# Attention and max-out layer on one core: weights loaded in another order, and the product of w2 and w_out built inside batch 0

## The chip, the cores and the metric

The kernel runs on one core of a Trainium2 chip. The metric is the device time of one execution in microseconds (us), the median of several runs. A core has a matrix engine (PE, with its weight loads PEld shown beside it), a vector engine (DVE), a scalar engine (ACT), a general engine (POOL) and a sync engine (SP) that here only issues transfers. Each engine works through its own list of instructions in order and waits at the head of that list until the data it needs is there. Transfers issued from SP, ACT and POOL are carried by 16 DMA engines.

## The reference

```python
scores = q @ k^T / sqrt(64)                     # batch 8, heads 8, 576 tokens, 64 wide
scores = where(block(i) >= block(j), scores, -1e9)   # blocks of 64 tokens, causal by block
attn   = exp(scores - max) / sum
x      = (attn @ v) with the heads side by side # 4608 tokens x 512
out    = maximum(x @ w1, x @ w2) @ w_out        # w1, w2: 512 x 1024, w_out: 1024 x 512
```

## The kernel before, in words

All products run in bf16 with sums in float32. The max-out layer is rewritten: maximum(x w1, x w2) = x w2 + maximum(x (w1 - w2), 0). The kernel therefore needs d = w1 - w2 (`d_sb`), and M = w2 w_out (`m_sb`), and computes out = x M + maximum(x d, 0) w_out.

The heads are taken as 32 pairs `p`, four pairs per batch; two pairs make a group `g`, whose q and k arrive in one transfer each (`load_qk`, 576 KB). For each group the kernel casts q and k to bf16, transposes them on PE (`transposes`, ps_qT and ps_kT), and copies them out on DVE and ACT. For each pair it then computes scores in pieces (`burst_...` in batch 0, `tile_0`, `tile_1`, `tile_2` later) into two PSUM buffers (`ps_s`), takes exp on ACT (`aT`), zeroes the masked corners with memsets (`mask`, on POOL mostly), multiplies with V (`av`, ps_o; "early" tokens 0 to 255 as `[0, 1]`, "late" ones as `[2, 3, 4]`), and divides by the sums on DVE. `x_out` transposes the result on PE and copies it into `xT`; from batch 1 on a DMA transpose does that instead.

The max-out layer is cut into units that PE works on between the pieces of attention. There are four kinds: `bT_unit` (8 transposes of w2, then one DVE copy into `bT_sb`; four units), `m_unit` (8 matmuls of 256 columns and a DVE copy into `m_sb`; eight units, the first four need the first half of w_out), `h_unit` (4 matmuls and a DVE maximum into `g`), and `y_unit` (12 matmuls into the output). `plan` lists the units in order, each with the tokens it needs. `fill(n)` issues units in that order until a budget of n is spent; a matmul of 512 columns costs 1, one of 256 costs 0.5, a transpose 0.25. `fill_of(g)` sets the budget of a group from the units that are ready. `warm_up(n)` issues n matmuls on zeros, with no result, that only keep PE running.

All other matrix products, transposes and `fill` units take their result from one pool of four PSUM buffers (`ps_m`), handed out in turn: a piece of work may begin only when the one four places before it has been copied out.

The order of everything in batch 0 (groups 0 and 1) and at the start of batch 1 (group 2, pairs 4 and 5) is written out by hand at the end of the program. From group 3 on a loop repeats one pattern: scores of the next pair, a fill, `av` of the pair two before, and so on.

V and the weights are loaded by POOL (`load_v`, `load_w`, `load_wo`), which also converts them to bf16, except w1, that arrives in float32. w2 has no buffer of its own: it lies in a part of `xT` that later batches fill. q and k are loaded by SP; `gated=True` puts a memset on POOL ahead of the transfer, so that it starts only when POOL has come to that point of its list. In the kernel before, POOL loads the first two chunks of V, a quarter of w1, a quarter of w2, the three late chunks of V, then the other quarters in pairs, then w_out, then V of batch 1, then the fourth q and k.

Of the kernel before, what the change touches and what calls it, by code (L numbers as in the profile page):

```python
# [8 lines left out]
FP32 = mybir.dt.float32  # L9
# [5 lines left out]
def kernel(  # L15
# [10 lines left out]
    nc = tc.nc  # L26

    B, H, S, D = q.shape
# [83 lines left out]
    def load_qk(g, queues, gated=False):  # L112
        b, u = divmod(g, GPB)
        for nm, src, queue in (("q", q, queues[0]), ("k", k, queues[1])):
            if queue is None:
                continue
            raws[nm, g] = t = raw.tile([P, 2, RPP * D], FP32, name=f"{nm}raw")
            if gated:
                nc.gpsimd.memset(t[:, 0, :1], 0.0)
            queue.dma_start(  # L120
                out=t[:],
                in_=src[b, 4 * u:4 * u + 4].rearrange(
                    "(s h) (p t) d -> (h p) s (t d)", h=2, t=RPP),
            )

    def cast(nm, g, parts):
        t = raws[nm, g].rearrange("p s (t d) -> p t s d", d=D)
        if (nm, g) not in qk_n:
            qk_n[nm, g] = qkn.tile([P, RPP, 2, D], BF16, name=f"{nm}n")
        n = qk_n[nm, g]  # L130
        for copy, j0, j1 in parts:
            copy(out=n[:, j0:j1], in_=t[:, j0:j1])  # L132

    def load_v(b, c):
        rows = min(P, S - c * P)
        nc.gpsimd.dma_start(  # L136
            out=vv_r[b % NV][P - rows:, c, :, :D],
            in_=v[b, :, c * P:c * P + rows, :].rearrange("h p d -> p h d"),
        )
# [3 lines left out]
    wor = moe_w_out.rearrange("(c p) f -> p c f", p=P)  # L143

    WB = 256
    w1_raw, w2_sb = {}, []
    for j in range(d_ff // WB):
        row, n = (1, j) if j < 3 else (3, 0)
        t0 = 3 * S - 3 * BLK + n * NDM * WB
        w2_sb.append(xT[:, row, t0:t0 + NDM * WB].rearrange("p (c f) -> p c f", c=NDM))  # L150

    def load_w(j, which=(0, 1)):
        fs = slice(j * WB, (j + 1) * WB)
        if 0 in which:
            w1_raw[j] = wraw.tile([P, NDM, WB], FP32, name="w1raw")
            nc.gpsimd.dma_start(out=w1_raw[j][:], in_=w1r[:, :, fs])
        if 1 in which:
            nc.gpsimd.dma_start(out=w2_sb[j], in_=w2r[:, :, fs])

    def diff_w(j):  # L160
        fs = slice(j * WB, (j + 1) * WB)
        nc.vector.tensor_sub(d_sb[:, :, fs], w1_raw[j][:], w2_sb[j])  # L162

    WH = d_model // 2

    def load_wo(i):
        ds = slice(i * WH, (i + 1) * WH)
        nc.gpsimd.dma_start(out=wo_sb[:, :, ds], in_=wor[:, :, ds])  # L168
# [8 lines left out]
    nc.vector.memset(zeros[:], 0.0)  # L177
    nc.scalar.activation(out=warm[:], in_=warm[:], func=AF.Exp)
    load_qk(1, (SP, SP))
    load_qk(2, (SP, None))  # L180
    make_identity(nc, ident)
    for r in range(NV):
        nc.vector.memset(vv_r[r][:, :, :, D:D + 1], 1.0)
# [6 lines left out]
    cast("k", 0, ((act, 0, 5), (dve, 5, RPP)))  # L190
    for c in range(2):
        load_v(0, c)
    load_w(0, (0,))
    cast("q", 1, ((pool, 7, RPP),))
    cast("k", 1, ((pool, 0, 7),))
    load_w(0, (1,))


    done_tokens = [0]
# [23 lines left out]
    def bT_unit(j):  # L223
        pt = ps_m.tile([P, 2, NDM, P], BF16, name="ps_bT", tag="m")
        for i in range(2):
            for c in range(NDM):
                nc.tensor.transpose(pt[:, i, c, :], w2_sb[j][:, c, i * P:(i + 1) * P], ident[:])
                if i == 1 and c == NDM - 1:
                    nc.vector.tensor_copy(
                        out=bT_sb[:, 2 * j:2 * j + 2, :],  # L230
                        in_=pt.rearrange("p i c d -> p i (c d)"))
                yield

    def m_unit(i, c):
        ds = slice(i * WH, (i + 1) * WH)
        pt = ps_m.tile([P, WH], FP32, name="ps_M", tag="m")
        for f in range(NFF):
            nc.tensor.matmul(  # L238
                pt[:], bT_sb[:, f, c * P:(c + 1) * P], wo_sb[:, f, ds],
                start=(f == 0), stop=(f == NFF - 1),  # L240
            )
            if f == NFF - 1:
                nc.vector.tensor_copy(out=m_sb[:, c, ds], in_=pt[:])
            yield
# [40 lines left out]
    def plan():  # L285
        def h(i, f):
            t0, w = spans[i]
            units.append((h_unit(i, f), t0 + w, w / SPAN, NDM))

        def y(i, s, last=False):  # L290
            t0, w = spans[i]
            if last:
                units.append((y_last(i, s), t0 + w, 0.333, 3 * NY))
            else:
                units.append((y_unit(i, s), t0 + w, 1.0, NY))

        for i in range(NSPAN):
            for f in range(NFF):
                h(i, f)
                if i == 0 and f % 2:  # L300
                    units.append((bT_unit(f // 2), 0, 0.25, 2 * NDM))
                if i > 2 and f % 2 == 0 and f // 2 < tiles[i - 1]:
                    y(i - 1, f // 2)
            if i == 1:
                for n in range(2 * NDM):
                    units.append((m_unit(n // NDM, n % NDM), 0, 0.5, NFF))
                for j in range(2):
                    for s in range(tiles[j]):
                        y(j, s)
        n = tiles[-1]  # L310
        for s in range(n):
            y(NSPAN - 1, s, s == n - 1)
# [25 lines left out]
    def warm_up(n):  # L338
        pw = ps_m.tile([P, SPAN], FP32, name="ps_w", tag="m")
        for _ in range(n):  # L340
            nc.tensor.matmul(pw[:], zeros[:, :P], zeros[:], start=True, stop=True)  # L341
# [4 lines left out]
    def transposes(nm, g, copies):  # L346
        n = qk_n.pop((nm, g))
        pts = [ps_m.tile([P, RPP, NP], BF16, name=f"ps_{nm}T", tag="m") for _ in range(2)]
        for j in range(RPP):
            for i in range(2):  # L350
                r = slice(i * NP, (i + 1) * NP)
                nc.tensor.transpose(  # L352
                    pts[i][:, j, :], n[r, j].rearrange("p s d -> p (s d)"), ident[r, r],
                )

        def copy_out(which=(0, 1), part=(0, NP), copy=None):
            p0, p1 = part
            for i in which:
                t = (qT_r if nm == "q" else kT_r)[(2 * g + i) % NT]
                (copy or copies[i])(  # L360
                    out=t[:, p0 * RPP:p1 * RPP].rearrange("q (p j) -> q p j", j=RPP),
                    in_=pts[i][:, :, p0:p1].rearrange("q j p -> q p j"),
                )
        return copy_out
# [12 lines left out]
    def pad_keys(p):  # L377
        nc.gpsimd.tensor_copy(
            out=kz_r[p % NT].rearrange("p (a c) -> p a c", c=BLK)[:, 0:3:2],
            in_=kT_r[p % NT][:, S - 3 * BLK:].rearrange("p (a c) -> p a c", c=BLK)[:, 0:3:2],  # L380
        )
# [31 lines left out]
    def burst_q1(p):  # L413
        burst(p, ((0, QCUT, 320), (1, QCUT, 192)), 384)

    def burst_q2(p):
        burst(p, ((1, 448, P), (2, QCUT, 320), (4, 512, BLK)), 896)

    def burst_q3(p):
        burst(p, ((3, 384, 192),), 1408)  # L420

    def masks_p(p, eng=None):
        for a in (0, 256):
            mask(p, a, eng)

    def masks_q(p, eng=None):
        for a in (1024, 1408):
            mask(p, a, eng)
# [160 lines left out]
    burst_p(1)  # L589
    warm_up(2)  # L590
    masks_p(1)
    for c in range(2, NCH):
        load_v(0, c)
    load_qk(2, (None, SP), gated=True)
    load_w(1)
    cq = transposes("q", 1, (dve, dve))
    burst_q1(0)
    ck = transposes("k", 1, (dve, dve))
# [15 lines left out]
    masks_p(3, nc.vector)  # L614
    burst_q2(0)
    av(2, [0, 1])
    warm_up(2)
    x_out(0, 0, 2, (act, act))
    av(3, [0, 1])
    diff_w(0)  # L620
    burst_q1(1)
    warm_up(2)
    cast("q", 2, ((pool, 0, RPP),))
    masks_q(0)
    load_w(2)
    burst_q2(1)
    x_out(1, 0, 2)
    warm_up(2)
    burst_q3(1)
    masks_q(1)  # L630
    load_w(3)
    fill(4)
    burst_q1(2)
    transposes("q", 2, (dve, act))()
    burst_q2(2)
    av(0, [2, 3, 4])
    burst_q3(2)
    masks_q(2)
    cast("k", 2, ((pool, 0, RPP),))
    load_wo(0)  # L640
    load_wo(1)
    av(1, [2, 3, 4])
    burst_q1(3)
    burst_q2(3)
    av(2, [2, 3, 4])
    transposes("k", 2, (dve, act))()
    burst_q3(3)
    masks_q(3)
    pad_keys(4)
    pad_keys(5)  # L650
    for c in range(NCH):
        load_v(1, c)
    load_qk(3, (SP, SP), gated=True)
    x_out(0, 2, NCH)
    fill(2)
    diff_w(1)
    outs = tile_0(4), tile_1(4)
    av(3, [2, 3, 4])
    region(*outs)
    x_out(1, 2, NCH)  # L660
    fill(4)
    diff_w(2)
    fill(2)
    region(tile_2(4), tile_0(5))
    fill(4)
    diff_w(3)
    fill(2)
    region(tile_1(5), tile_2(5))
    fill(4)
    fill(2)  # L670
    cast("q", 3, ((pool, 0, RPP),))
    cast("k", 3, ((pool, 0, RPP),))
    n = fill_of(GPB)
# [86 lines left out]
```

The softmax here doesn't subtract the row's maximum and nothing guards it: scores larger than these inputs give would overflow.

## Time and profile before

| what | value |
|---|---|
| time, median of 3 runs | 260.99 us (260.82 to 261.92) |
| span of the profiled execution | 259.2 us |
| PE busy | 244.8 us (94%) |
| DVE, ACT, POOL busy | 137.6, 141.3, 109.8 us |
| TensorE clock granted | 1.0 of full speed throughout |
| read from HBM, written to it | 34.60 MB, 9.44 MB |

Busy time is the time in which an engine had an instruction at work. PE is the busiest by far, so the places where PE is not busy, or is busy with matmuls on zeros, are where time can be found. The matmuls overlap in the pipeline, so that the mean length of one in the table of groups (0.2 to 0.4 us) is longer than the step from one to the next.

### The profile page before, as it was taken

What the parts mean: (1) busy time and instruction counts of PE and PEld (TensorE: products, weight loads), DVE (VectorE), ACT (ScalarE), POOL (GpSimd) and SP (SyncE); (2) the same over time, 40 slices, a digit from 0 to 9 for tenths busy, and PEclk for the clock granted to TensorE, in tenths of its full rate; (3) what the DMA queues carried; (4) which work ended last, traced back from release to release, by engine and by line L of the source; (5) the groups of instructions that cost most, each with busy time, mean ns of one, the idle gap of its engine ahead of it and who ended that gap; (6) DMA issues with size and microseconds to landing.
All of it is one profiled execution on the core that took longest, in us unless ns stands there. A gap on an engine that the chain in (4) does not pass through costs nothing.

```text
span 259.2 us, 7161 instructions
## 1 busy us (share of the span) xinstructions
PE 244.8 (94%) x2949; PEld 139.4 (54%) x2983; DVE 137.6 (53%) x301; ACT 141.3 (55%) x198; POOL 109.8 (42%) x274
## 2 busy tenths in 40 slices
PE   8688799999999999999999999999999999999995
PEld 3346566856555545454646464646464655444444
DVE  4967996646584518451855185518550853453200
ACT  2798552766665766576657665776577431100111
POOL 2987914475638163816381638263823010000000
DMA  7999998789579995998599949984986122202122
GB/s 245 317 204 310 194 241 146 280 73 275 111 184 250 135 195 136 238 149 215 129 236 139 179 163 239 141 208 139 90 106 116 44 51 83 83 0 81 43 104 99
DMA packets 71265, 41.30 MB, mean 159 GB/s; under 512 B 53568, under 2 KB 58048, under 8 KB 71232
## 3 DMA queue, kind: packets, MB, share of 16 engines
q1 hardware_dynamic: 28544, 31.27, 41.4%
q0 software_dynamic: 42272, 8.92, 38.2%
q10 hardware_dynamic: 416, 0.66, 0.7%
q8 instruction: 23, 0.38, 0.6%
q14 instruction: 10, 0.08, 0.1%
HBM read 34.60 MB, written 9.44 MB: 170 GB/s over the span
## 4 chain that ended last, share of the span: by engine, by line
PE 85%; DMA 5%; POOL 3%; issue 2%; ACT 2%; DVE 1%; POOLq 0%; ACTq 0%
PE ps_y L257 35%; PE ps_h L215 22%; PE ps_o L479 10%; PE ps_s L371 8%; DMA qraw<-in_q_dram 5%; PE ps_M L238 3%; PE ps_qT L352 2%; PE ps_kT L352 2%; POOL vv L136 1%; ACT aT L395 1%; PE ps_y L272 1%; DVE qn L132 1%; PE ps_w L341 1%; PE ps_s L389 1%; POOL wo_sb L168 1%
## 5 line engine op out<-in xcount | busy, mean ns | idle before, releaser
L395 ACT ACTIVATE aT<-ps_s 128x1024 bf16<-128x1024 f32 (+2 forms) x100 | 95.9, 996 | 28.6 <-PE ps_s L371 26.6
L215 PE MATMUL ps_h<-xT,d_sb 128*128 128x512 bf16 (+3 forms) x306 | 67.4, 357 | 2.7 <-DVE d_sb L162 1.2
L257 PE MATMUL ps_y<-wo_sb,g 128*128 128x512 bf16 x275 | 69.1, 379 | 0.4 <-issue 0.3
L220 DVE TENSOR_SCALAR g<-ps_h 128x512 bf16<-128x512 f32 (+3 forms) x80 | 50.8, 636 | 30.2 <-PE ps_h L215 28.4
L400 POOL MEMSET aT<- 64x128 bf16 x124 | 22.4, 199 | 85.1 <-ACT aT L395 84.4
L485 DVE RECIPROCAL rec<-ps_o 128x4 f32<-128x4 f32 (+1 forms) x64 | 12.0, 188 | 62.7 <-PE ps_o L479 61.9
L215 PEld LDWEIGHTS <-d_sb 128*128 128x128 bf16 x320 | 29.1, 98 | 30.1 <-issue 2.7
L479 PEld LDWEIGHTS <-aT 128*128 128x128 bf16 x960 | 37.2, 98 | 13.5 <-issue 0.8
L262 ACT COPY y<-ps_y 128x512 f32<-128x512 f32 x31 | 18.2, 587 | 44.8 <-PE ps_y L257 32.6
L257 PEld LDWEIGHTS <-g 128*128 128x128 bf16 x280 | 25.9, 98 | 29.7 <-issue 1.9
L479 PE MATMUL ps_o<-vv,aT 128*128 128x65 bf16 x960 | 39.8, 194 | 0.0
L257 PE MATMUL ps_y<-m_sb,xT 128*128 128x512 bf16 x128 | 36.5, 380 | 1.2 <-issue 0.8
L136 POOL DMA_DIRECT2D vv<-in_v_dram x40 | 33.6, 847 | 1.6 <-issue 1.2
L371 PE MATMUL ps_s<-qT,kT 64*128 64x64 bf16 (+6 forms) x344 | 31.0, 280 | 1.9 <-ACT kT L360 0.7
L486 DVE TENSOR_TENSOR xp<-ps_o,rec 128x256 bf16<-128x256 f32 (+1 forms) x64 | 31.4, 491 | 2.2
L360 ACT COPY qT<-ps_qT 128x576 bf16<-128x576 bf16 (+1 forms) x17 | 10.3, 614 | 20.0 <-PE ps_qT L352 20.0
L132 POOL CAST qn<-qraw 128x1152 bf16<-128x1152 f32 (+1 forms) x16 | 17.0, 1061 | 8.7 <-DMA qraw<-in_q_dram 8.7
L257 PEld LDWEIGHTS <-xT 128*128 128x128 bf16 x140 | 12.2, 98 | 15.1 <-issue 3.5
L371 PEld LDWEIGHTS <-kT 64*128 64x128 bf16 x344 | 12.2, 94 | 11.0 <-issue 6.2
L132 POOL CAST kn<-kraw 128x1152 bf16<-128x1152 f32 (+1 forms) x15 | 17.1, 1141 | 1.4 <-DMA kraw<-in_k_dram 1.3
L360 ACT COPY kT<-ps_kT 128x576 bf16<-128x576 bf16 x15 | 9.6, 639 | 14.6 <-PE ps_kT L352 14.6
L207 POOL COPY g<-g 128x512 bf16<-128x512 bf16 x8 | 4.9, 613 | 20.7 <-DVE g L220 20.3
(57 smaller groups left out, 160.8 us busy)
## 6 DMA issues: line engine op xcount, KB each, us to landing
qraw<-in_q_dram SPq DMA_DIRECT2D x16, 576.0 KB, 4.1
out_dram<-y SPq DMA_DIRECT2D x35, 256.0 KB, 3.2
kraw<-in_k_dram SPq DMA_DIRECT2D x15, 576.0 KB, 5.4
vv<-in_v_dram POOLq DMA_DIRECT2D x32, 128.0 KB, 5.2
w1raw<-in_moe_w_dram POOLq DMA_DIRECT2D x4, 512.0 KB, 8.7
xT<-in_moe_w_dram POOLq DMA_DIRECT2D x4, 256.0 KB, 9.1
wo_sb<-in_moe_w_out_dram POOLq DMA_DIRECT2D x2, 512.0 KB, 9.0
kraw<-in_k_dram ACTq DMA_DIRECT2D x1, 576.0 KB, 5.5
```

Of the source, the lines that this page charges most:

```text
L132: copy(out=n[:, j0:j1], in_=t[:, j0:j1])
L136: nc.gpsimd.dma_start(out=vv_r[b % NV][P - rows:, c, :, :D], in_=v[b, :, c * P:c * P + rows, :].rearrange("h p d -> p h d"),)
L215: nc.tensor.matmul(pt[:, :w], d_sb[:, c, f * P:(f + 1) * P], xT[:, c, t0:t0 + w], start=(c == 0), stop=(c == NDM - 1),)
L220: nc.vector.tensor_scalar_max(g[:, f, m:m + w], pt[:, :w], 0.0)
L257: nc.tensor.matmul(py[:], lhs, rhs, start=(n == 0), stop=(n == len(terms) - 1),)
L262: (dve if i < 2 else act)(out=y[:], in_=py[:])
L360: (copy or copies[i])(out=t[:, p0 * RPP:p1 * RPP].rearrange("q (p j) -> q p j", j=RPP), in_=pts[i][:, :, p0:p1].rearrange("q j p -> q p j"),)
L371: nc.tensor.matmul(ps[:, hh, col:col + w], kT[r, k0:k0 + P], qT[r, q0:q0 + w], start=True, stop=True,)
L395: nc.scalar.activation(out=aT_r[p % NA][:, :, a0:a0 + w], in_=ps[:, :, :w], func=AF.Exp, scale=scale,)
L400: (eng or nc.gpsimd).memset(aT_r[p % NA][BLK:, :, a0:a0 + BLK], 0.0)
L479: nc.tensor.matmul(po[:, gi, hh, :], a[:, hh, a0:a0 + P], vv[:, c, h0 + 2 * hh, :], start=(mm == 0), stop=(mm == n_mm - 1),)
L486: nc.vector.tensor_mul(xp[:, :, ts[0]:ts[0] + n, p % 2].rearrange("q s t d -> q t s d"), po[:, :, :, :D], rec[:, :n].to_broadcast([P, n, 2 ...
```

## The change

The change reorders the loads and the work of batch 0. POOL now loads, after the first two chunks of V, the whole of w2 in two halves of 1 MB read each, half of w_out, the late chunks of V, the other half of w_out, and two quarters of w1; then come the third q and k (both gated behind the masks of pair 1), the last two quarters of w1, three chunks of V of batch 1, the fourth q and k, and the last two chunks of V. The units of w2's transposes and of M move to the head of the plan, in front of all others. They take the place of three pairs of matmuls on zeros, and stand between the scores and the late values of batch 0. The subtractions d = w1 - w2 and the first h units move behind M.

```diff
+    WC = d_ff // 2
+    w2_sb = [xT[:, row, 3 * S - 3 * BLK:3 * S - 3 * BLK + NDM * WC].rearrange(...) for row in (1, 3)]
+    def load_w2(i):
+        nc.gpsimd.dma_start(out=w2_sb[i], in_=w2r[:, :, i * WC:(i + 1) * WC])
...
-    load_qk(2, (SP, None))
...
-    load_w(0, (0,))
+    load_w2(0)
     cast("q", 1, ((pool, 7, RPP),))
     cast("k", 1, ((pool, 0, 7),))
-    load_w(0, (1,))
+    load_w2(1)
...
+        for n in range(NFF // 2):
+            units.append((bT_unit(n), 0, 0.25, 2 * NDM))
+        for n in range(2 * NDM):
+            units.append((m_unit(n // NDM, n % NDM), 0, 0.5, NFF))
...
     masks_p(1)
+    load_wo(0)
     for c in range(2, NCH):
         load_v(0, c)
-    load_qk(2, (None, SP), gated=True)
-    load_w(1)
+    load_wo(1)
+    load_w1(0)
+    load_w1(1)
...
     av(2, [0, 1])
-    warm_up(2)
+    fill(2)
     x_out(0, 0, 2, (act, act))
     av(3, [0, 1])
-    diff_w(0)
     burst_q1(1)
-    warm_up(2)
-    cast("q", 2, ((pool, 0, RPP),))
+    fill(2)
     masks_q(0)
-    load_w(2)
     burst_q2(1)
     x_out(1, 0, 2)
-    warm_up(2)
+    fill(2)
     burst_q3(1)
     masks_q(1)
-    load_w(3)
-    fill(4)
+    load_qk(2, (SP, SP), gated=True)
+    fill(2)
     burst_q1(2)
-    transposes("q", 2, (dve, act))()
     burst_q2(2)
+    fill(4)
+    fill(4)
+    burst_q3(2)
+    load_w1(2)
+    masks_q(2)
+    burst_q1(3)
+    load_w1(3)
+    fill(4)
+    fill(4)
+    burst_q2(3)
     av(0, [2, 3, 4])
...
     burst_q3(3)
     masks_q(3)
+    cast("q", 2, ((pool, 0, RPP),))
+    cast("k", 2, ((pool, 0, RPP),))
+    for c in range(3):
+        load_v(1, c)
+    load_qk(3, (SP, SP), gated=True)
+    for c in range(3, NCH):
+        load_v(1, c)
+    av(1, [2, 3, 4])
+    av(2, [2, 3, 4])
+    x_out(0, 2, NCH)
+    diff_w(0)
+    fill(4)
+    fill(4)
+    transposes("q", 2, (dve, act))()
+    av(3, [2, 3, 4])
+    fill(4)
+    transposes("k", 2, (dve, act))()
     pad_keys(4)
     pad_keys(5)
...
     diff_w(1)
...
     x_out(1, 2, NCH)
     fill(4)
+    region(tile_0(4), tile_1(4))
+    fill(4)
     diff_w(2)
-    fill(2)
     region(tile_2(4), tile_0(5))
     fill(4)
     diff_w(3)
-    fill(2)
+    fill(4)
     region(tile_1(5), tile_2(5))
     fill(4)
```

More of the change, by code (lines that the diff above doesn't have):

```diff
@@ L145, with load_w1 @@
     WB = 256
[L146 to L158, printed above, removed]
+    w1_raw = {}
+    WC = d_ff // 2
+    w2_sb = [
+        xT[:, row, 3 * S - 3 * BLK:3 * S - 3 * BLK + NDM * WC].rearrange("p (c f) -> p c f", c=NDM)
+        for row in (1, 3)]
+    def load_w1(j):
+        w1_raw[j] = wraw.tile([P, NDM, WB], FP32, name="w1raw")
+        nc.gpsimd.dma_start(out=w1_raw[j][:], in_=w1r[:, :, j * WB:(j + 1) * WB])
+    def load_w2(i):
+        nc.gpsimd.dma_start(out=w2_sb[i], in_=w2r[:, :, i * WC:(i + 1) * WC])
     def diff_w(j):
-        fs = slice(j * WB, (j + 1) * WB)
-        nc.vector.tensor_sub(d_sb[:, :, fs], w1_raw[j][:], w2_sb[j])
+        n = j * WB % WC
+        nc.vector.tensor_sub(
+            d_sb[:, :, j * WB:(j + 1) * WB], w1_raw[j][:], w2_sb[j * WB // WC][:, :, n:n + WB])
     WH = d_model // 2
@@ L225, in bT_unit @@
         for i in range(2):
+            f = 2 * j + i
             for c in range(NDM):
-                nc.tensor.transpose(pt[:, i, c, :], w2_sb[j][:, c, i * P:(i + 1) * P], ident[:])
+                nc.tensor.transpose(pt[:, i, c, :], w2_sb[f // (NFF // 2)][:, c, f % (NFF // 2) * P:(f % (NFF // 2) + 1) * P], ident[:])
                 if i == 1 and c == NDM - 1:
@@ L299, in plan @@
                 h(i, f)
-                if i == 0 and f % 2:
-                    units.append((bT_unit(f // 2), 0, 0.25, 2 * NDM))
                 if i > 2 and f % 2 == 0 and f // 2 < tiles[i - 1]:
@@ L304, in plan @@
             if i == 1:
-                for n in range(2 * NDM):
-                    units.append((m_unit(n // NDM, n % NDM), 0, 0.5, NFF))
                 for j in range(2):
@@ L616 @@
     av(2, [0, 1])
-    warm_up(2)
+    fill(2)
     x_out(0, 0, 2, (act, act))
     av(3, [0, 1])
-    diff_w(0)
     burst_q1(1)
-    warm_up(2)
-    cast("q", 2, ((pool, 0, RPP),))
+    fill(2)
     masks_q(0)
-    load_w(2)
     burst_q2(1)
     x_out(1, 0, 2)
-    warm_up(2)
+    fill(2)
     burst_q3(1)
     masks_q(1)
-    load_w(3)
+    load_qk(2, (SP, SP), gated=True)
+    fill(2)
+    burst_q1(2)
+    burst_q2(2)
     fill(4)
-    burst_q1(2)
-    transposes("q", 2, (dve, act))()
-    burst_q2(2)
-    av(0, [2, 3, 4])
[L637 to L646, printed above, removed]
+    fill(4)
[7 more added lines that the diff above has]
+    burst_q2(3)
+    av(0, [2, 3, 4])
     burst_q3(3)
     masks_q(3)
+    cast("q", 2, ((pool, 0, RPP),))
[15 more added lines that the diff above has]
+    transposes("k", 2, (dve, act))()
     pad_keys(4)
     pad_keys(5)
[L651 to L654, printed above, removed]
-    fill(2)
     diff_w(1)
-    outs = tile_0(4), tile_1(4)
-    av(3, [2, 3, 4])
-    region(*outs)
     x_out(1, 2, NCH)
     fill(4)
+    region(tile_0(4), tile_1(4))
+    fill(4)
     diff_w(2)
-    fill(2)
     region(tile_2(4), tile_0(5))
@@ L666 @@
     diff_w(3)
-    fill(2)
+    fill(4)
     region(tile_1(5), tile_2(5))
     fill(4)
-    fill(2)
     cast("q", 3, ((pool, 0, RPP),))
```

## The prediction

> **What bounds the kernel now.** I read the page's head first, then stretches of the span, then the order of PE and the waits of the stretches where PE is not full. The page:
>
> ```profile
> span 259.2 us, 7161 instructions
> PE 244.8 (94%) x2949; PEld 139.4 (54%) x2983; DVE 137.6 (53%) x301; ACT 141.3 (55%) x198; POOL 109.8 (42%) x274
> ...
> PE   8688799999999999999999999999999999999995
> ```
>
> PE is the bound, and its gaps lie in the first six or seven slices, some 40 us. The busy time by stretch (time; then busy us of PE, PEld, DVE, ACT, POOL; clock; share and GB/s of the DMA engines):
>
> ```profile
> 15.50:26.00 10.50, 9.54 (x202) 6.53 (x201) 7.56 (x19) 9.65 (x14) 8.05 (x15) 1.00 1.35 272
> 26.00:34.50 8.50, 6.10 (x99) 4.37 (x96) 7.76 (x15) 4.96 (x7) 6.12 (x17) 1.00 1.56 188
> 34.50:44.00 9.50, 8.80 (x104) 6.73 (x105) 7.59 (x16) 2.71 (x5) 2.92 (x7) 1.00 1.15 173
> 44.72:56.28 11.56, 11.51 (x191) 8.38 (x193) 6.44 (x17) 7.55 (x10) 6.29 (x20) 1.00 0.80 202
> 56.28:67.41 11.13, 10.81 (x184) 6.44 (x180) 6.71 (x15) 7.55 (x10) 6.17 (x15) 1.00 0.99 186
> ```
>
> PE idles 0.96, 2.40 and 0.70 us in the first three rows: 4.06 us between 15.5 us and 44.72, where group 3 begins. Before 15.5 PE's list is the same in both kernels. From group 3 on PE idles about 2%, nearly all of it "issue". PE's own waits between 26 and 41 us:
>
> ```profile
> PE ps_xe L517 <- DVE xp L486: 1.2, 1, 1.2
> PE ps_h L215 <- DVE d_sb L162: 1.2, 2, 0.6
> ...
> PE ps_qT L352 <- POOL qn L132: 0.6, 1, 0.6
> ```
>
> PE waits for attention's division (late values follow each other with nothing between), for d (w1 comes last), and for the fourth q. M comes only after that, when PE is already full:
>
> ```profile
> 15.53 0.59 PE L341 MATMUL ps_w<-zeros 128*128 128x512 bf16 x2
> ...
> 16.89 0.60 PE L341 MATMUL ps_w<-zeros 128*128 128x512 bf16 x2
> ...
> 41.42 1.58 PE L238 MATMUL ps_M<-wo_sb,bT_sb 128*128 128x256 bf16 x13
> ```
>
> The third zero pair runs at 17.87. All real work is the same in both kernels, so the gain can only be zero work removed and idle time filled.
>
> [...] the third k, issued at 14.15 behind POOL's loads, took 8.0 us to land; a q of the same 576 KB issued at 42.30, when little else ran, took 3.7. [...] w2's transposes replace the zero matmuls; but the trace has them at 219 ns each, eight in 0.54 us to the next start, with the clock at 1.00, so I charge nothing. [...] I count steps from start to start and not lengths.
>
> **The ceiling.** Steps from the order of PE before: 8 transposes of w2 0.54 us; an M matmul 0.123 (12 in 1.48); a zero matmul 0.216; a y matmul 0.215 (6 in 1.30).
> At the start of group 3 the old kernel has done 25 of 64 M matmuls; the new order has done all 64 and 2 y matmuls. That lead is 39 x 0.123 + 2 x 0.215 = 5.23 us. The old PE was busy 25.16 of the 29.22 us to 44.72. The new work is 25.16 - 6 x 0.216 + 5.23 = 29.09 us. With no idle time group 3 would start at 44.6 with 5.23 us less to do: a ceiling of 1.30 + 4.06 = 5.36 us. From pair 10 on, the two orders hold the same fills per piece, so what is won by then stays won.
>
> **w2 and w_out early.** In the old trace the second V chunk landed at 12.7 us, with the third q (landed 10.9) beside it. Without that q I put it at 11.7. For 1 MB read of weights the queue took 1.7 us (second w_out half, 32.5 to 34.2), 2.6 (first) or 2.7 (last quarters of w1 and w2, 27.2 to 29.9). At 2.4 each, w2 lands at 14.1 and 16.5, the first w_out half at 18.9; at 12.7 and 2.7 each it is 20.8. PE wants the halves of w2 at 15.5 and 17.9, and w_out at 19.75. So I take no wait; the upper end is 1.0 us. The late V follows (0.9 us a chunk, 18.3 to 20.0 before): about 21.6, wanted at 24.4. The second w_out half at about 24 to 25.5, wanted at 27.5. None waits.
>
> **bT and M between the scores.** DVE copies of bT (0.69 each) come between divisions; the last is done near 20.0, and M reaches those columns at 20.5. ACT is the busy engine here (9.65 of 10.5), and now gets scores a little later: exp for pair 3 ends near 25.9, as before (26.0). That costs PE nothing, since it has M to do. Small waits for a division and for PSUM: 0.2 us.
>
> **From 27 to 40 us.** Here I laid PE's new list and DVE's beside each other with the old steps: on DVE a division (reciprocal and product) 0.76 us, x copies 0.6, each of four subtractions 1.22, an M copy 0.42, a q or k copy 0.75, a maximum 0.43; on PE late values 0.84, an M unit 0.98, an h pair 0.9. What PE then waits for:
> Late values of pair 3: their PSUM is that of M's fifth unit, which DVE copies only after the first subtraction (28.5 to 29.7): ready at 30.1, wanted at 29.75, 0.4.
> Transposes of x for group 1: those values divided, and M's seventh unit copied: 0.15.
> M's last unit: its buffer is the third k's, copied at 33.1, wanted at 32.7: 0.45.
> First h units: x copies stand behind the second subtraction on DVE, done 34.9: 0.1.
> Scores of pair 5: two score buffers, an exp of 0.97 us each, so PE waits for ACT: 0.6.
> Last quarter's h units: fourth subtraction done at 39.4, wanted at 39.2: 0.2.
> The sum is 1.9, with the 0.2 above 2.1 us, against 4.06 in the old kernel.
>
> **Third and fourth q, k and V.** POOL reaches the gate of the third q and k after pair 1's exp, at 19.8. With 8 us to land as in the old case, q is there at 27.8 and k at about 29; casts (1.15 each) end at 29.0 and 30.4; PE wants them at 29.5 and 32. The wait is nothing, up to 1.75 us if they queue behind all the weights. Behind the casts on POOL stand V of batch 1 (0.84 us an issue) and the fourth q, k: issued at 33 in place of 31.34. Its landing was 7.6 and 9.1 us later; at 40.6 and 42.1, cast by 43.3, against PE's wish at 43 and 45. V was there at 43.6, and is wanted at about 47. No wait in the forecast.
>
> **Group 3 and 4, given back.** The lead makes `fill_of` smaller: the fills there were 39 M and 12 y matmuls (7.38 us) and 30 y (6.45), and are 20 y in each (4.30). Of the old 11.56 and 11.13 us PE keeps 8.5 and 9.0, and ACT still has 7.55. At the end of a group ACT has a copy 0.64, two exps 0.97 and a corner 0.27 = 2.85 us in line, PE only 0.55 of scores and 6 fills of 0.215, then a first score piece of 0.25: 2.1. So a wait of about 0.75 at group 5; at group 4 the x transposes (0.5) cover most. I take 0.8 in all; the bounds are 0 and 1.6.
>
> **Sum.** 5.36 - 2.1 - 0.8 = 2.46 us; 260.99 - 2.46 = 258.5.
>
> **Rivals.**
> First, everything is hidden: DVE keeps up and groups 3 and 4 do not wait. Idle of 0.9 us stays, 5.36 - 0.9 = 4.5, so 256.5. For it: POOL's cast of the third q leaves a contested time, and PE waits in groups 3 and 4 have so far been nil. Against: DVE is 7.76 of 8.5 us busy already in that stretch.
> Second, late loads: w_out at 20.8 costs 1.0 us, and the fourth q and k 1.1 more, so 260.6, no change that counts. For it: the DMA engines are loaded throughout, 11 MB in 32 us. Against: the bytes ahead of w_out are fewer than what preceded it.
> Third, slower: POOL's list stalls at the third q's cast. If q lands at 30, its cast ends at 31.2 (1.75 us of PE), and V of batch 1 is issued until 36.6; with its old 13 us to land, it comes at 49.6, 1.6 us after it is wanted. With w_out's 1.0: 258.5 + 4.35 = 262.9. For it: POOL works in order, and everything behind that cast waits. Against: the 13 us held weights ahead in the queue that are now gone.
>
> **How the numbers follow.** Forecast 0.58, everything hidden 0.12, late loads 0.19, stall 0.11. The first two are faster by over 0.5% (under 259.7): 0.70. Late loads are within: 0.19. Stall is slower (over 262.3): 0.11. The range reaches from the first rival to a little beyond the late loads, 256.4 to 260.9, and leaves out the stall.
>
> **What would show it.** Right: the zero pairs gone; ps_M between 19.7 and 34 us; group 3's first scores at 46 to 47; PE idle near 2 us between 15.5 and there, released by DVE and ACT; a short wait of ps_s on ACT at the start of group 5; the loop's steady part unchanged. Wrong: PE waiting for a DMA, first ps_M on w_out, or ps_qT on POOL's cast; ps_o waiting for V of batch 1; or PE waits in groups 3 and 4 well above 1 us.

## The result, and the profile after

| | before | after |
|---|---|---|
| time, median | 260.9 us (4 runs, 260.73 to 261.92) | 263.6 us (4 runs, 263.17 to 264.53) |
| ratio | | 1.010 (95% interval 1.0062 to 1.0138) |
| span of the profiled execution | 259.2 us | 262.8 us |

The forecast was 258.5 us and faster; the kernel became 2.7 us slower, outside the range of 256.4 to 260.9. The page after, by its head, the row of PE in 40 slices, and a row that the page of the kernel before did not have, the granted clock:

```profile
span 262.8 us, 7139 instructions
...
PE 245.1 (93%) x2943; PEld 138.8 (53%) x2977; DVE 137.5 (52%) x301; ACT 141.8 (54%) x198; POOL 108.4 (41%) x273
...
PE   7578769998999999999999999999999999999995
...
PEclk9999998999999999999999999999999999999999
```

Six matmuls on zeros are gone, and PE is busy for 0.3 us more. Slices of low PE busy time reach to about 40 us as before, and in the seventh (39.4 to 46.0 us) the clock was below full. Busy time by stretch (time; PE, PEld, DVE, ACT, POOL; clock; DMA share and GB/s):

```profile
15.50:26.00 10.50, 8.74 (x124) 6.43 (x122) 5.56 (x14) 7.30 (x10) 4.61 (x13) 1.00 1.62 218
26.00:33.60 7.60, 6.25 (x149) 5.30 (x147) 5.43 (x13) 2.15 (x3) 1.54 (x3) 1.00 0.97 337
33.60:38.66 5.06, 2.60 (x50) 1.95 (x46) 3.06 (x6) 0.64 (x1) 3.36 (x4) 1.00 0.16 23
38.66:42.28 3.62, 3.62 (x25) 1.72 (x25) 2.15 (x7) 2.00 (x3) 2.88 (x9) 0.54 1.68 133
42.28:51.80 9.52, 9.25 (x107) 6.21 (x107) 9.09 (x18) 5.75 (x8) 3.52 (x11) 1.00 0.79 165
51.80:60.72 8.92, 8.60 (x159) 5.36 (x162) 4.86 (x12) 6.72 (x9) 5.62 (x14) 1.00 0.76 267
60.72:70.34 9.62, 8.94 (x173) 5.42 (x169) 6.18 (x14) 7.56 (x11) 6.59 (x17) 1.00 1.37 224
```

PE's idle time to the start of group 3 (51.80) is 1.76 + 1.35 + 2.46 + 0.27 = 5.84 us, where the old kernel had 4.06 and the forecast 2.1. On top, in the fourth row PE is "busy" throughout at 0.54 of its clock, which is 3.62 x 0.46 = 1.67 us lost. The waits of PE between 12 and 75 us:

```profile
PE ps_kT L352 <- POOL kn L132: 1.9, 1, 1.9
PE ps_o L479 <- DVE m_sb L243: 1.2, 1, 1.2
...
PE ps_M L238 <- DMA wo_sb<-in_moe_w_out_dram: 0.9, 1, 0.9
PE ps_s L371 <- ACT aT L451: 0.9, 2, 0.5
PE ps_bT L227 <- DMA xT<-in_moe_w_dram: 0.7, 1, 0.7
PE ps_M L238 <- ACT kT L360: 0.6, 1, 0.6
```

The largest in this trace is the third k. POOL, which casts it, stood still for it 4.4 us, and V of batch 1 and the fourth q and k stood behind it (POOL's timeline):

```profile
29.77 1.14 POOL L132 CAST qn<-qraw 128x1152 bf16<-128x1152 f32 x1 [1.67 <-DMA qraw<-in_q_dram]
35.30 1.15 POOL L132 CAST kn<-kraw 128x1152 bf16<-128x1152 f32 x1 [4.38 <-DMA kraw<-in_k_dram]
36.39 1.77 POOL L136 DMA_DIRECT2D vv<-in_v_dram  x2
```

That k was issued at 21.12 and took 14.0 us. In the old kernel the third k, issued at 14.15, took 8.0. The lower clock shows in PE's timeline: the same six score matmuls take 1.04 us at 38.66 (clock 0.50) and 0.61 at 51.80 (1.00).

```profile
38.66 1.04 PE L371 MATMUL ps_s<-qT,kT 64*128 64x512 bf16 x6
...
51.80 0.61 PE L371 MATMUL ps_s<-qT,kT 64*128 64x512 bf16 x6
```

The sum of the profiled run: ceiling 5.36, less idle 5.84, less clock 1.67, less 1.55 given back from group 3 to the start of group 5 (below), is -3.7 us; the two spans differ by 3.6. The median of the four runs is 0.9 us better than this profiled run (264.53): the other three had a mean clock of 1.00 and took 263.17 to 263.80. So the clock adds to the profiled run, but it is not what makes the median slow.

### The profile page after: what moved, and what is told of

Its sections match the earlier page's. It is cut to its first block, busy times and chain, and to the rows that moved or that the text cites. A ratio compares the mean times of both kernels' runs of the same rounds, so it can differ in the third digit from the quotient of the medians.

```text
span 262.8 us, 7139 instructions
## 1 busy us (share of the span) xinstructions
PE 245.1 (93%) x2943; PEld 138.8 (53%) x2977; DVE 137.5 (52%) x301; ACT 141.8 (54%) x198; POOL 108.4 (41%) x273
## 4 chain that ended last, share of the span: by engine, by line
PE 81%; DMA 10%; ACT 4%; issue 2%; POOL 1%; SPq 0%; ACTq 0%; POOLq 0%
PE ps_y L257 34%; PE ps_h L214 24%; PE ps_o L479 10%; PE ps_s L371 7%; DMA kraw<-in_k_dram 5%; DMA xT<-in_moe_w_dram 3%; ACT aT L395 3%; PE ps_kT L352 2%; DMA qraw<-in_q_dram 2%; PE ps_qT L352 2%; PE ps_y L272 1%; PE ps_s L389 1%; ACT kT L360 1%; POOL vv L136 1%; POOL kn L132 0%
## 5 line engine op out<-in xcount | busy, mean ns | idle before, releaser
L214 PE MATMUL ps_h<-xT,d_sb 128*128 128x512 bf16 (+3 forms) x307 | 68.1, 361 | 1.4 <-issue 1.0
L479 PE MATMUL ps_o<-vv,aT 128*128 128x65 bf16 x960 | 39.6, 194 | 1.2 <-DVE m_sb L243 1.2
L371 PE MATMUL ps_s<-qT,kT 64*128 64x64 bf16 (+6 forms) x344 | 31.8, 285 | 2.6 <-ACT aT L451 0.9
L360 DVE COPY kT<-ps_kT 128x576 bf16<-128x576 bf16 (+2 forms) x19 | 12.9, 685 | 1.9 <-PE ps_kT L352 1.9
```

Of the source, the lines that this page charges most:

```text
L214: nc.tensor.matmul(pt[:, :w], d_sb[:, c, f * P:(f + 1) * P], xT[:, c, t0:t0 + w], start=(c == 0), stop=(c == NDM - 1),)
L360: (copy or copies[i])(out=t[:, p0 * RPP:p1 * RPP].rearrange("q (p j) -> q p j", j=RPP), in_=pts[i][:, :, p0:p1].rearrange("q j p -> q p j"),)
L371: nc.tensor.matmul(ps[:, hh, col:col + w], kT[r, k0:k0 + P], qT[r, q0:q0 + w], start=True, stop=True,)
L479: nc.tensor.matmul(po[:, gi, hh, :], a[:, hh, a0:a0 + P], vv[:, c, h0 + 2 * hh, :], start=(mm == 0), stop=(mm == n_mm - 1),)
```

## The experiments

All stand beside runs of the kernel before on the same chip (medians 260.9 to 261.0). The edits of e1 to e4, e7 and e8 are made in the changed kernel; e5 builds on e1.

**e1, the third q at the start again.**

```diff
     load_qk(1, (SP, SP))
+    load_qk(2, (SP, None))
...
-    load_qk(2, (SP, SP), gated=True)
+    load_qk(2, (None, SP), gated=True)
```

> One part undone: the third q is loaded at the very start again, ungated, as in the kernel before; the third k stays behind the masks of pair 1. Theory A (the DMA engines ran below their rate from 9 to 12 us once the third q was taken out of the opening, and the third k then lands at 35.1 us because it queues with everything that was pushed back): 590 KB leave the crowded stretch, about 1.5 us at the 390 KB/us read there, so the third k lands near 33.5, w2's first half still near 16.5 to 17.5, and the time falls by 1 to 2.5 us against the changed kernel (263.6), to about 261 to 262.5. Theory B (the third k is late because its gate opens only at 20.6 us, whatever else is in the queue): the third k still lands after 34.5 and the time stays within 0.7 us of 263.6.

Measured: 260.83 us, ratio to before 0.9992 (0.9975 to 1.0009). The third k was issued at 20.84 and landed at 31.0, not 35.1. The waits of PE from 12 to 75 us:

```profile
PE ps_M L239 <- DMA wo_sb<-in_moe_w_out_dram: 1.3, 1, 1.3
...
PE ps_s L372 <- ACT aT L452: 0.9, 2, 0.5
...
PE ps_o L480 <- DMA vv<-in_v_dram: 0.7, 1, 0.7
PE ps_M L239 <- ACT kT L361: 0.3, 1, 0.3
```

PE no longer waits for the third k, and the whole 2.7 us is back, though PE now waits longer for w_out and also for V. The 1.2 us wait for a copy of M is gone as well: w1's first quarter, for which the first subtraction waits, lands at 29.8 in place of 31.2. Where one transfer stands in the queue is worth the result of the whole change. The gain is above Theory A's 1 to 2.5; that the freed 1.5 us of transfer moved the landing by 4.2 us was not expected.

**e2, the gate of the third q and k earlier.**

```diff
     load_wo(1)
+    load_qk(2, (SP, SP), gated=True)
     load_w1(0)
...
     masks_q(1)
-    load_qk(2, (SP, SP), gated=True)
```

> One part moved: the gate of the third q and k stands right after the issue of w_out's second half, ahead of w1, in place of behind the masks of pair 1 (issue near 16 us, not 20.7). Theory A (the third k's landing sets the stretch from 33 to 42 us, and its gate and the four quarters of w1 decide it): the third k lands between 24 and 28 us, PE no longer waits for it (1.9 us) or for its copy (0.6), the clock stays at 1.00, and the time falls by 2.5 to 4.5 us from 263.6, to 259 to 261; the price is w_out's first half up to 1 us later. Theory B (the waits for w2, w_out and d set the time, and the third k only comes on top of them by chance): PE's wait moves to w_out and d, and the time falls by under 1 us.

Measured: 262.97 us, ratio 1.006 (1.0037 to 1.0082). In the profile, a run of 261.28 us, the third q landed at 23.5, k at 26.3, and PE did not wait for them; it waited 0.8 us for w_out and 0.7 for late V. But of 20 runs only 6 had a mean clock of 1.00 (median 261.2); 11 had 0.993 or 0.994 (median 263.2), and three had 0.987 (264.9 to 266.5) and are not in the ratio. Theory A is right on the landing, near on the time in the runs at full clock (259 to 261 expected), and wrong that the clock stays. The profile is of a run at full clock, so where the clock falls in this version was not seen.

**e3, zero matmuls while PE waits.**

```diff
     fill(4)
+    warm_up(9)
     transposes("k", 2, (dve, act))()
```

> Nine matmuls on zeros (about 1.9 us at the 0.216 us step) are added in the changed kernel ahead of the third k's transposes, where PE idles 1.9 us for that k. Theory A (the granted clock falls to half for 3.6 us because PE idled just before, worth 1.7 us in a run where it happens): the clock is 1.00 in every run, first scores of group 3 come 1 to 1.7 us earlier than the 51.8 of the profiled run, and the median falls by 0.3 to 1.5 us, since only one of four runs of the changed kernel shows a mean clock below 1.00. Theory B (the clock is not a matter of the idle time there): the mean clock still falls in some runs and the median stays within 0.3 us, or rises by the zeros that are not hidden.

Measured: 264.20 us, ratio 1.0117 (1.0084 to 1.0151): no gain. In its profile PE idled 1.74 of the 4.00 us from 29 to 33, and the clock was at half before PE came to the zeros:

```profile
29.00:33.00 4.00, 2.26 (x49) 1.89 (x47) 2.45 (x4) 0.64 (x1) 1.14 (x1) 0.94 0.94 325
33.00:36.00 3.00, 3.00 (x18) 1.83 (x16) 1.29 (x4) 0.00 (x0) 1.75 (x2) 0.50 0.10 29
```

So the zeros, which start at 34.9, came too late: the clock fell behind a wait of 1.3 us for a copy of M, before PE reached them. The other three runs had mean clocks of 0.998 to 1.00 and took 263.3 to 265.2, no less than the changed kernel. That fits Theory B. This run does not say what keeping PE busy would have been worth, only that this place did not do it.

**e4, the first subtraction later.**

```diff
-    diff_w(0)
     fill(4)
     fill(4)
     transposes("q", 2, (dve, act))()
+    diff_w(0)
```

> The first subtraction stands behind two M units and the third q's transposes in place of ahead of them, so that the copies of M no longer wait on the vector engine for w1. Theory A (the third k's landing at 35.1 us ends this stretch, and the wait ahead of it, 1.2 us of the late values of pair 3 for a copy of M, is swallowed by it): the wait at 31.7 goes, the wait for the third k grows by as much, and the time stays within 0.7 us of 263.6. Theory B (each wait adds to the time by itself): the time falls by about 1.2 us, to 262.4.

Measured: 263.16 us, ratio 1.0088 (1.0053 to 1.0122), 0.4 us below the changed kernel. The 1.2 us wait is gone in the profile, a wait of 1.4 us for the third k remains. The time stays within 0.7 us, as Theory A has it, but its reason is not shown: the wait for the k became shorter and not longer, since the gate opened 0.6 us earlier in that run and the k landed at 33.1. And all four runs had a mean clock of 0.993, where three of the changed kernel's four had 1.00. In the two traces, each with one fall of the clock, group 3 starts at 50.07 here and at 51.80 there. So this run does not decide between the theories.

**e7, w1 behind the third k.** The last two quarters of w1 are issued behind the casts. The question is whether transfers issued at about the same time as the k, or after it, hold it up.

```diff
     burst_q3(2)
-    load_w1(2)
...
     burst_q1(3)
-    load_w1(3)
...
     cast("k", 2, ((pool, 0, RPP),))
+    load_w1(2)
+    load_w1(3)
```

> In the changed kernel the last two quarters of w1 are issued behind the casts of the third q and k, so that these two transfers no longer share the DMA engines with them. Theory A (the third k takes 14 us [...]): the third k lands 2 to 3 us sooner, near 32.5, PE's wait for it falls below 0.7 us, and the time falls by 1 to 2.5 us from 263.6. Theory B (the third k waits only for what was issued ahead of it: V, w_out, the first half of w1 and the third q): it still lands near 35, and the time does not fall.

Measured: 262.80 us, ratio 1.0068 (1.0051 to 1.0085). The third k was issued at 20.32 and landed at 31.9, 3.2 us before the changed kernel's. Of that, 0.8 us is the earlier issue; the k took 11.6 us in place of 14.0. In e3, e4 and e8, which leave these loads as they are, it took 12.6 to 13.8, so 1.0 to 2.4 us are this edit's. The two transfers that were moved had been issued at 20.82 and 24.72 on POOL's queue, one 0.3 us ahead of the k (21.12, on SP's) and one 3.6 us after it; which of the two held it up was not tried apart. Theory A is right on the landing, wrong on the time: PE's wait for the k is gone, yet the time fell by only 0.8. A wait that had not existed took its place:

```profile
PE ps_s L389 <- POOL kz L378: 1.8, 1, 1.8
```

POOL now issues two quarters of w1 (1.5 us), besides V of batch 1 and the gate of the fourth q and k, ahead of the padded keys that the first corner scores need.

**e8 and e5, what groups 3 and 4 give back.** The middle fills of these two groups are halved, so that more is left for the end; e8 is the changed kernel, e5 is e1.

```diff
-        lo, hi = max(3, n // 18), n * 2 // 9
+        lo, hi = max(3, n // 18), n // 9 if g < 5 else n * 2 // 9
```

In the changed kernel, PE's timeline at the start of groups 4 and 5 showed these two lines (the scores' last part, with the wait ahead of it in brackets):

```profile
61.62 0.40 PE L371 MATMUL ps_s<-qT,kT 64*128 64x64 bf16 x4 [0.47 <-ACT aT L451]
...
71.24 0.40 PE L371 MATMUL ps_s<-qT,kT 64*128 64x64 bf16 x4 [0.47 <-ACT aT L451]
```

> The fills of groups 3 and 4 are moved as in e5, in the changed kernel itself. Theory A (what groups 3 and 4 give back stands apart from the late loads): the time falls by the same 0.5 to 1.3 us as e5 against e1, to 262.3 to 263.1. Theory B (it is part of one chain with the late loads): no fall, or a different one.

> The third q early as in e1, and in groups 3 and 4 the two fills in the middle are halved, so that the fill at the end of the group is larger (10 y matmuls' worth in place of 6). Theory A (groups 3 and 4 give back about 1.5 us, because the scores at the start of groups 4 and 5 wait 0.5 us each for exps still in line on the scalar engine, with too little fill at the end of the group): the waits of 0.47 us at the start of groups 4 and 5 go, and the time falls by 0.5 to 1.3 us from e1's 260.8, to 259.5 to 260.3. Theory B (the scalar engine's work per group, 7.55 us of 9, sets the pace wherever the fill stands): the wait moves to the middle of the group and the time stays within 0.4 us of e1.

Measured: e8 262.43 us, ratio 1.0057 (1.0038 to 1.0075), 1.2 below the changed kernel; e5 260.06 us, ratio 0.9961 (0.9947 to 0.9975), 0.8 below e1. Both 0.47 us waits are gone in both, and the times are as Theory A has them. But the traces do not show that the whole gain comes from there. A new wait stands in group 3, for POOL's cast of the fifth q, where the middle fill was made smaller (e8, then e5):

```profile
53.35 0.44 PE L352 MATMUL ps_qT<-ident,qn 64*128 64x64 bf16 x18 [0.94 <-POOL qn L132]
50.52 0.44 PE L353 MATMUL ps_qT<-ident,qn 64*128 64x64 bf16 x18 [0.62 <-POOL qn L132]
```

From the first scores of group 3 to those of the second pair of group 5, the changed kernel takes 23.68 us and e8 23.60; e1 takes 23.67 and e5 23.27. In e8 nearly all the difference between the two traces lies before group 3, where nothing was edited: group 3 starts at 49.71, with no fall of the clock and 4.69 us of idle PE in place of 5.84. In that trace PE does not wait for the third k (landed at 33.6), but 2.0 us for w_out and 1.4 for a copy of M. So which of the late loads holds PE differs from run to run of the same code, and why e8's median is 1.2 lower stays open in part.

**e6, the third q behind the first V.** As e1, but q is gated behind the two V chunks.

```diff
         load_v(0, c)
+    load_qk(2, (SP, None), gated=True)
     load_w2(0)
```

> The third q is loaded right behind the first two chunks of V (issue near 8.1 us), not at the start and not behind pair 1's masks; the third k as in the changed kernel. Theory A (the DMA engines are at 110 GB/s from 9 to 12 us in the changed kernel, and the third q fits into that gap): V lands by 12.5 and PE does not wait for it (e1: 0.7 us), w2's first half lands by 17, the third k by 32, the time is 259.8 to 261. Theory B (any early third q only delays w2 and w_out by its own 1.5 us): PE's waits for w2 and w_out rise to 2.5 us or more together, and the time is above 261.3.

Measured: 261.63 us, ratio 1.0031 (1.0016 to 1.0046). The third k landed at 32.1 and w2's first half at 17.4, near what Theory A said, but the second chunk of V, issued ahead of that q, landed only at 14.8 (12.0 in the changed kernel), and PE waited 1.7 us for it. Right behind that wait, at 14.97, the clock fell to half for 3.4 us in this trace. Neither theory had that. The gap from 9 to 12 us is not free: V is in flight there (its second chunk was issued at 7.2 and landed at 12.0 in the changed kernel).

**e9 and e10, versions.** e9 is e5 with the edit of e4. e10 is e9 with the third k's gate right behind the second half of w_out.

> e5 (third q at the start, fills of groups 3 and 4 moved to the end) and the first subtraction moved as in e4. In e5's profile the late values of pair 3 wait 0.5 us for a copy of M behind that subtraction, and nothing later swallows it, since PE no longer waits for the third k. Theory A (once the third k is out of the way, each wait counts): 0.3 to 0.6 us below e5, ratio to the kernel before 0.993 to 0.996. Theory B (the vector engine is so full there that the wait moves to the x copies or the second subtraction): within 0.2 us of e5.

Measured: 259.39 us, ratio 0.9941 (0.992 to 0.9963), faster than both kernels. It is 0.67 us below e5, a little more than expected; the intervals of e5 and e9 overlap. The wait for M's copy is gone, but the trace does not put the gain there: group 3 starts at 47.25 and in e5 at 47.20, because PE waits 0.6 us for the division of x and 0.4 each for w2 and w_out instead, which is near to Theory B. What is shorter comes later: 22.58 us from group 3 to the second pair of group 5, against 23.27, without the wait for the fifth q's cast. That q landed at 48.4, 0.8 us sooner than in e5; whether the edit did that was not tried. Head and PE row of its page:

```profile
span 257.1 us, 7137 instructions
...
PE 243.9 (95%) x2942; PEld 138.7 (54%) x2977; DVE 137.4 (53%) x301; ACT 141.6 (55%) x198; POOL 108.8 (42%) x272
...
PE   8689989999999999999999999999999999999995
```

> e9 with the third k's gate right behind the issue of w_out's second half, as in e2. Theory A (POOL's list is still late behind the third k's cast: in e5 the fifth q's cast comes 0.6 us late for group 3): the third k lands 3 us sooner, this wait goes, and the time falls by 0.3 to 0.8 us from e9. Theory B (the third k then shares the DMA engines with w_out and late V, and PE waits for those): no fall, and as in e2 the clock falls in some runs.

Measured: 262.40 us, ratio 1.0027 (1.0008 to 1.0045); Theory B. The early k took the place of w_out: PE waited 2.6 us for w_out in the profile, and of 22 runs 10 had full clock (260.4 to 261.3) and 12 had 0.993 (262.4 to 263.7), with nothing between. The stretches show PE busy for 1.36 of 4.00 us and the clock at 0.61 after it:

```profile
20.00:24.00 4.00, 1.36 (x21) 0.97 (x22) 1.22 (x2) 2.45 (x4) 1.35 (x4) 1.00 1.80 230
24.00:28.00 4.00, 4.00 (x28) 2.52 (x26) 0.85 (x2) 1.45 (x2) 0.87 (x2) 0.61 1.41 282
```

## Why the prediction was wrong

**The ceiling** is not where it failed. The zero matmuls went, the sum of the profiled run closes with 5.36 in it, and e9 realises 1.5 to 1.6 us of it.

**"Third and fourth q, k and V" failed.** It gave the third k 8 us "as in the old case"; it took 14.0. In the old case, at 14.15, the three late chunks of V, a quarter of w2 and one of w1 had not landed. Here the gate opened later (20.6; 19.8 forecast) with the three late chunks of V, both halves of w_out (the first landed at 21.7) and two quarters of w1 not yet landed, and two more quarters of w1 to follow. The forecast took the 8 us over and left out that a transfer can also be delayed by what is issued after it. e6 shows that: a chunk of V took 7.7 us with a q issued 1.0 us after it, and 4.8 in the changed kernel (4.2 to 4.8 in the six traces without that q). e7 fits: 1.0 to 2.4 us of the k's time went with two transfers, of which one had been issued after it. The third rival named the right chain (POOL stalls at a cast, all behind it waits) and put it on q; the upper end of the term, "1.75 us if they queue behind all the weights", comes near the wait of PE (1.87) but was left out of the sum. That this rival's 262.9 lies near the measured time is in part luck: 1.6 us of it is a wait for V of batch 1, and PE did not wait for that. e1 shows what this crowd costs as a whole: with the third q out of it, the loss is gone. It does not show the third k's share by itself, since w1 comes sooner there too, and in e8's trace the same crowd holds PE at w_out instead.

**"w2 and w_out early" was mis-sized.** Forecast landings 14.1, 16.5 and 18.9, with 20.8 as the upper end for w_out; measured 16.3, 18.9 and 21.7. The term of 0 to 1.0 us was 1.66 (0.71 + 0.95). The working let one transfer follow the other at 2.4 us per MB from V's end at 11.7. Two things were off. The 2.4 leans on a landing that was misread: the second half of w_out, issued at 25.23, took 9.9 us and landed at 35.1, not 34.2, so its 1.7 us were about 2.6, like the other two. And V did end at 12.0, but after it the rate was not there at once (one stretch of the kernel before, then two of the changed kernel):

```profile
9.00:12.00 3.00, 1.58 (x45) 1.12 (x47) 2.89 (x7) 2.80 (x6) 2.96 (x8) 1.00 1.86 253
9.00:12.00 3.00, 1.58 (x46) 1.07 (x48) 2.95 (x7) 2.80 (x5) 2.86 (x8) 1.00 1.37 110
12.00:22.00 10.00, 7.66 (x116) 4.80 (x117) 6.58 (x20) 7.67 (x12) 6.96 (x14) 1.00 1.55 186
```

From 9 to 12 us only 110 GB/s were written, against 253 in the kernel before, where the third q ran there. From 12 to 22 us it is 186 (bf16 written, twice as much read). The first 1 MB landed 4.3 us after V, and the next two 2.6 and 2.8 us apart. They had been issued at 8.07, 10.23 and 11.60, so from 11.60 to 16.3 us all three were in flight together.

**"From 27 to 40 us"** named the waits for copies of M rightly and made them too short. The late values of pair 3 waited 1.19, not 0.4, because the first subtraction waited 1.09 us for w1, landed at 31.2; M's last unit 0.59, not 0.45. The 0.6 us that the scores of pair 5 were to wait for ACT did not come in this trace, but in e1's, with 0.49.

**The clock was missing altogether.** I charged nothing for the transposes in place of zeros, on the ground that the old trace ran them at full clock. That ground held where they stand (1.00 from 15.5 to 26 us); the clock fell later, after a stretch in which PE waited. In the profiled run it was at 1.00 up to 38.64 us and then at 0.50 for 3.40 us:

```profile
35.24:38.64 3.40, 1.55 (x36) 1.26 (x36) 1.67 (x2) 0.64 (x1) 3.34 (x4) 1.00 0.15 10
38.64:42.04 3.40, 3.40 (x25) 1.71 (x24) 1.93 (x7) 1.94 (x2) 2.90 (x9) 0.50 1.73 124
```

PE was busy for 1.55 of the 3.40 us before the fall, and its longest single wait there was 1.9. The falls in e3, e4, e6 and e10 also last 3.4 us, and PE was busy for 1.17 to 1.67 us of the 3.4 before them. A low busy share is not all of it, for in e7 from 36.2 to 39.6 us (1.61 of 3.40) and in e1 from 10.6 to 14.0 (1.56) no fall followed. What else decides, and why the clock falls in some runs only of the same kernel, no run shows. Of 103 runs of the kernel before on the chips of the experiments none had a mean clock under 0.998.

**"Group 3 and 4, given back"** was right in kind and small in size: 0.8 forecast, with 1.6 as the upper end. Groups 3 and 4 took 70.34 - 51.80 = 18.54 us, where the old ones took 22.69 less 5.23 of fills, 17.46: 1.08 us; the wait in the first scores of group 5 adds 0.47. Together 1.55. In the traces e9 has 1.1 us of it back (23.67 us in e1, 22.58 in e9, up to the second pair of group 5).

## What to carry to other kernels

Loads moved earlier move other loads later (the third k, issued at 21.12, landed at 35.1 us; in the old order, issued at 14.15, at 22.1), and the one to look at is the one that an engine must touch before it can issue anything else: here a cast of k on POOL, which stood still 4.4 us for it with V of batch 1 waiting behind. Price a transfer by all that is in flight in its time, on every queue and also issued after it (7.7 us for the chunk of V in e6, 4.2 to 4.8 without the q), not by its time in the old order (8.0 us for the third k, which then took 14.0). Where fill work is pulled forward, ask which later stage lived on it, and leave the rest of that stage's fill where its longest line of exps ends; then look at what the fill had covered where it is taken away (in e8 a cast of q, 0.9 us).

## What the runs showed of the hardware that was not expected

The granted clock fell to half while PE was at work for part of the time: in five traces (the changed kernel, e3, e4, e6, e10) PE was busy for 1.17 to 1.67 of the 3.4 us before the fall, the longest single gap among them was 2.6 us, and each fall lasted 3.4 us. What one fall costs is not the same everywhere. In e10 the runs with a mean clock of 0.993 take 1.9 us more in the median than those at full clock (262.5 and 260.6), with nothing between 261.3 and 262.4. In e6 the five runs with a mean clock of 0.992 or 0.993 lie at 261.0 to 263.2, among those at full clock (261.2 to 263.2).

A chunk of V (256 KB read, in rows of 256 bytes) landed 4.2 to 4.8 us after its issue in the six traces that have no third q beside it, and 7.7 us after it in e6, where a q of 576 KB was issued 1.0 us later on another queue.
